# Attention scores of batches 1 to 7: zero-padded queries on all 128 rows in place of paired half-row matmuls

## The chip, the cores and the metric

One core of a Trainium2 chip runs the whole program. The metric is the device time of one execution in microseconds (us), a median of several runs. TensorE (PE) does the matmuls, ScalarE (ACT) the exponentials and part of the copies out of PSUM, VectorE (DVE) the rest of those and the elementwise work, GpSimd (POOL) casts and starts part of the DMAs, SyncE (SP) starts the other DMAs.

## What is computed

Eight batches, 12 heads, 448 positions, 64 numbers a head. Attention comes first, with one more term in the denominator; its output, with the heads side by side, is the input x (448 x 768 a batch) of a gated convolution.

```python
scores = scale * np.matmul(q, k.transpose(0, 1, 3, 2))
e = np.exp(scores - m)
attn = e / (np.sum(e, axis=-1, keepdims=True) + np.exp(-m) + 1e-09)
x = np.matmul(attn, v)                       # then (B, S, H * D)
proj = x @ w_proj                            # x1, x2, x3, 768 columns each
x2_conv = np.fft.irfft(np.fft.rfft(x2, n=S, axis=1) * H, n=S, axis=1)
out = (x1 * x2_conv * x3) @ w_out
```

## The kernel before

**Attention (L592 to L721).** The unit of work is a pair of heads, number i = 6 b + hp, so 48 in all. The two heads of a pair lie on the partitions: head u on partitions 64u to 64u+63 of `qT` and `kT`, which hold the transposed queries (448 columns a pair) and keys (four blocks of 128 columns a pair). Both are double-buffered by batch (`b % 2`). Keys are handled in four *turns* t. In turn 0 one block holds the last 64 keys of both heads, in a block-diagonal layout, so one matmul over all 128 rows gives the scores of both (L606). In turns 1 to 3 each head has 128 keys of its own, and each needs a matmul over only its 64 partitions (L604): two half-row matmuls a turn, into the two halves of one PSUM buffer `sc`. There are two such buffers. ACT takes the exponential of a whole turn (L612, L617), then TensorE multiplies by the values (L649, L654), VectorE normalises (L667 to L669), and x is transposed, by TensorE (L703) or by a DMA (L693).

**Turns in pairs.** For batches 1 to 7, turns 1 to 3 are issued two at a time by `both` (L631): of the sequence of all turns 1 to 3, each even one is joined to the one before it, so that four half-row matmuls follow each other. Such a task takes both `sc` buffers. Turn 0 also waits, in the plan, for turn 2 of the pair of heads before it. Batch 0 issues each turn alone.

**Dense part (`dense`, L724).** For each batch: folding of x on VectorE (L747 to L763), projection of the folded x2 (L781), its spectrum (L808), products with the filter's spectrum (L822, L828), the gates x1 and x3 (L854, 12 groups of 6 matmuls, copied out at L866 and L869), the inverse transform (L888), and the output projection (L949) with its copies (L961) and stores (L968).

**Input.** Batches 0 and 1 are *staged*: SP loads q, k and v in float32, VectorE (the first) or GpSimd (the others) casts q and k (L301, L295), GpSimd casts v (L308) and the shared rows (L323, L326), TensorE transposes (`turn`, L332 to L339), and VectorE copies the results to `qT` and `kT` (L356, L348). Batches 2 to 7 are *loaded*: GpSimd starts DMAs that cast on the way (q at L376, k at L384 and L386, v at L398) and then copies two blocks of v (L406, 64 partitions x 384 each); SP starts the transposing DMAs into `qT` and `kT` (L410, L415). GpSimd also starts the loads of the filter (L487 to L491) and of the weights (L582, L587), in the order of `GATES` (L168).

**Order of work.** Each engine executes its own instructions in order. That order is written by a planner (`Plan`, L42). Every task has an engine, a cost, a wanted time, what it needs and makes, and ring buffers that it takes and gives. When an engine is free in the plan's clock, the first task in order of wanted time that can start is placed next. Wanted times of attention come from `tau` (L235): 3.5 us a pair of heads in batch 0, 5.5 in batch 1, and `PERIOD` / 6 after that, from `BASE2`. Those of the dense part come from `span` (L732), which spreads a batch's work over `PERIOD`, from `READY0` and `READY1` for the first two batches. Loads of a batch from 2 on are wanted 40 us before its attention (L371). The plan decides order alone; on the chip the semaphores decide the time.

Of the kernel before, what the change touches and what calls it, by code (L numbers as in the profile page):

```python
# [15 lines left out]
BF16 = mybir.dt.bfloat16  # L16
I32 = mybir.dt.int32

B, H, S, DH = 8, 12, 448, 64
# [22 lines left out]
class Plan:  # L42
# [14 lines left out]
    def add(self, eng, cost, want, emit, need=(), make=(), take=(), give=(), dma=0.0, after=0.0):  # L57
        self.tasks.append((want, len(self.tasks), eng, cost, emit, need, make, take, give, dma, after))
# [87 lines left out]
def kernel(  # L146
# [11 lines left out]
    nc = tc.nc  # L158
# [4 lines left out]
    SLOT1 = 5.5  # L163
    BASE2 = 77.0
    READY1 = 80.0
    READY0 = 35.0
    BPS = 18.0
    GATES = ((1, ("cq", 4)), ("F", ("cv", 7)), (0, ("cv", 9)), (2, ("cv", 10)), ("O", ("cv", 11)))  # L168
    STEP = 1.5
# [2 lines left out]
    const = ctx.enter_context(tc.tile_pool(name="const", bufs=1))  # L172
# [27 lines left out]

    kT = [const.tile([128, NHP, 4, 128], BF16, name=f"kT{i}") for i in range(2)]
    qT = [const.tile([128, NHP, S], BF16, name=f"qT{i}") for i in range(2)]
    vn = [const.tile([128, NHP, 7, DH + 1], BF16, name=f"vn{i}") for i in range(2)]
    vr = [const.tile([128, NHP, 2, DH + 1], BF16, name=f"vr{i}") for i in range(2)]
    ks = const.tile([128, NHP, 128], BF16, name="ks")
# [2 lines left out]
    er = [const.tile([128, S + REM], BF16, name=f"er{i}") for i in range(2)]  # L208
# [20 lines left out]
        }  # L229
    )  # L230
    add = plan.add
    ATT0, SLOT0, PERIOD = 6.0, 3.5, 44.5
    BASE = 31.0

    def tau(i, frac=0.0):  # L235

        if i < NHP:
            return ATT0 + SLOT0 * (i + frac)
        if i < 2 * NHP:
            return BASE + SLOT1 * (i + frac - NHP)  # L240
        return BASE2 + (i + frac - 2 * NHP) * PERIOD / NHP
# [348 lines left out]
    T = {}  # L590

    def attention(i):  # L592
        b, hp = divmod(i, NHP)
        P = T.setdefault(i, {})
        P["e"] = [None] * 4
        def scores(t):
            if t or b:
                P["sc", t] = sc = psc.tile([128, 2, 512], F32, name="sc")
            else:
                P["sc", t] = sc = phy.tile([128, 1, 512], F32, name="sc0", tag="hy")  # L600
            if t:
                for u in range(2):
                    c = slice(64 * u, 64 * u + 64)
                    nc.tensor.matmul(sc[:, u, 0:S], kT[b % 2][c, hp, t, :], qT[b % 2][c, hp, :])  # L604
            else:
                nc.tensor.matmul(sc[:, 0, 0:S], kT[b % 2][:, hp, 0, :], qT[b % 2][:, hp, :])  # L606

        def exps(t):
            sc = P["sc", t]
            if t:  # L610
                P["e"][t] = e = es[(3 * i + t - 1) % 6]
                nc.scalar.activation(  # L612
                    e[:, 0 : 2 * S].rearrange("p (u n) -> p u n", u=2), sc[:, :, 0:S], AF.Exp, scale=SCALE
                )
            else:
                P["e"][t] = e = er[i % 2]
                nc.scalar.activation(e[:, 0:S], sc[:, 0, 0:S], AF.Exp, scale=SCALE)  # L617

        P["scores"] = scores
        for t in range(4):  # L620
            w = tau(i, t / 4)
            ring = "sc" if t or b else "hy"
            if t == 0 or b == 0:
                add("PE", 0.4 if t else 0.19, w, lambda t=t: scores(t),
                    need=[("kT", i), ("qT", i)] + ([("S", i - 1, 2)] if b else []),
                    make=[("S", i, t)], take=[(ring, ("S", i, t))])
            elif (3 * i + t) % 2 == 0:

                old = (i, t - 1) if t > 1 else (i - 1, 3)

                def both(pair=(old, (i, t))):  # L631
                    for j, n in pair:
                        T[j]["scores"](n)

                add("PE", 0.61, tau(old[0], old[1] / 4), both, need=[("kT", old[0]), ("qT", old[0]), ("kT", i), ("qT", i)],
                    make=[("S",) + old, ("S", i, t)], take=[("sc", ("S",) + old), ("sc", ("S", i, t))])
            add("ACT", 0.93 if t else 0.56, w - 1.0, lambda t=t: exps(t), need=[("S", i, t)],
                make=[("e", i)], take=[("e" if t else "er", (i, t))], give=[(ring, ("S", i, t))])

        def attn_out(hf):  # L640
            e = P["e"]
# [35 lines left out]
        for hf in range(2):  # L677
            w = tau(i, 1.1 + 0.4 * hf)
            add("PE", 0.48, w, lambda hf=hf: attn_out(hf),
                need=[("e", i), ("ones", b % 2), "pads"] + ([("v", i), ("vr", b)] if b < NSTAGED else [("vn", b), ("vr", b)]),  # L680
                make=[("V", i, hf)], take=[("hy" if hf and b == 0 else "op", ("V", i, hf))], give=done)
            add("DVE", 0.78, w - 0.5, lambda hf=hf: norm(hf),
                need=[("V", i, hf)] + ([("X", NHP * (b - 1) - 1)] if b >= 2 else []),
                make=[("xb", i)], give=[("hy" if hf and b == 0 else "op", ("V", i, hf))])
# [29 lines left out]
        w = tau(i, 1.7)  # L714
        on_act = 4 <= i < 6
        old = [("G", b - 2)] if b >= 2 else []
# [7 lines left out]
    def dense(b):  # L724

        L = {}
        spread = PERIOD if b < n_batches - 1 else 36.0
        ready = tau(NHP * (b + 1), 1.0) if b > 1 else (READY0, READY1)[b]
        lag = 2.5
# [279 lines left out]
    with (  # L1009
        tc.tile_pool(name="tabs", bufs=1) as tp,  # L1010
        tc.manual_schedule(engines={E.PE, E.Pool, E.DVE, E.Activation, E.SP}),
    ):
        zero1 = tp.tile([128, 1], F32, name="zero1")
        warm = tp.tile([128, 1], F32, name="warm")
        add("DVE", 0.1, -20.0, lambda: nc.vector.memset(zero1, 0.0), make=["zero1"])
        add("POOL", 1.1, -20.0, count, make=["count"])
        add("POOL", 0.6, -19.0, lambda: make_identity(nc, ident_bf), make=["ident"])
        add("DVE", 2.8, -19.0, phases, need=["count"], make=["phases"])

        def blank(to):  # L1020
            nc.scalar.copy(to, zero1[0 : to.shape[0], :].to_broadcast(list(to.shape)))

        def spin():

            t = phy.tile([128, 512], F32, name="spin", tag="hy")
            for _ in range(SPIN):
                nc.tensor.matmul(t[:, 0:128], ident_bf, ident_bf)

        add("PE", 4.0, -20.0, spin, need=["ident"], make=["spin"], take=[("hy", "spin")], give=[("hy", "spin")])
        add("ACT", 1.6, -20.0, lambda: blank(ks[:].rearrange("p g c -> p (g c)")), need=["zero1"], make=["zero ks"])  # L1030

        add("ACT", 0.8, -18.0, lambda: blank(vr[0][:].rearrange("p g u d -> p (g u d)")), need=["zero1"], make=[("zero vr", 0)])
        add("ACT", 0.6, -17.0, sines, need=["phases"], make=["sines"])
        add("ACT", 1.5, -16.0, lambda: nc.scalar.activation(warm, zero1, AF.Exp), need=["zero1", "sines"])

        def pads():
            for e in es:
                nc.gpsimd.memset(e[:, 2 * S :], 0.0)
            for e in er:
                nc.gpsimd.memset(e[:, S:], 0.0)  # L1040

        add("POOL", 0.8, 7.0, pads, make=["pads"], after=4.5)

        def ones(i):
            nc.gpsimd.memset(vn[i][:, :, :, DH : DH + 1], 1.0)
            for u in range(2):
                nc.gpsimd.memset(vr[i][64 * u : 64 * u + 64, :, u, DH : DH + 1], 1.0)

        add("DVE", 0.4, 20.0, lambda: nc.vector.memset(vr[1], 0.0), make=[("zero vr", 1)], after=12.0)
        for i in range(2):  # L1050
            add("POOL", 0.7, (6.0, 24.0)[i], lambda i=i: ones(i), need=[("zero vr", i)], make=[("ones", i)],
                after=(4.5, 16.0)[i])
        for b in range(n_batches):
            if b < NSTAGED:
                staged(b)
            else:
                loaded(b)
        add("DVE", 0.5, tau(NHP * NSTAGED) - 30.0, lambda: nc.vector.memset(kn[:, :, 0, :], 0.0),
            need=[("c" + x, g) for x in "kqv" for g in range(NHP * NSTAGED - NHP, NHP * NSTAGED)], make=["zero kn"])
        for n, (part, key) in enumerate(GATES):  # L1060
            load, size = {
                "F": (filter_load, 4.5), "O": (wout_load, 8.0),
            }.get(part, (lambda part=part: wproj_load(part), 8.0))
            add("POOL", 1.6 if part == "F" else 0.95, 12.0 + 3 * n, load,
                need=[key] + (["ft", "bps"] if part == "F" else []),
                make=[{"F": "filt", "O": "wout"}.get(part, ("w", part))],
                take=[("yT", "F")] if part == "F" else [], dma=size)
        more_tables()
        filter_spectrum()
        for i in range(n_batches * NHP):  # L1070
            attention(i)
        for b in range(n_batches):
            dense(b)
        plan.run()
# [30 lines left out]
```

## Time and profile before

| what | value |
|---|---|
| median of three runs | 404.11 us (402.27 to 405.47) |
| profiled execution, its own time | 402.27 us |
| its span, first to last instruction | 400.5 us |
| mean granted TensorE clock | 0.987 |
| half-row score matmuls (L604) | 288, busy 43.0 us |
| full-row score matmuls (L606) | 48, busy 17.8 us |
| exponentials of turns 1 to 3 (L612) | 144, mean 923 ns, busy 127.8 us |
| time that DVE waited in all for TensorE at L667 | 49.6 us |
| longest single wait of ACT for a score at L612 | 3.9 us |

How to read the profile: a busy time is the union of an engine's instructions; PEld is TensorE's weight loads, which overlap matmuls. A group is written as line, engine, operation, output<-input and its shape. In a stage table, a row gives the stretch, its length, each engine's busy time with its number of instructions in brackets, and then the granted clock, the share of the DMA engines and their rate. In a timeline a row gives the start and the length of several instructions of one kind merged (x12 is twelve of them). A row of waits gives who waited, for whom, the total in us, the number of waits and the longest. Matmul lengths are modelled, and a matmul overlaps the next one, so start times say more than lengths.

### The profile page before, as it was taken

The numbers are of one execution on the slowest core, as the hardware profiler recorded it, in microseconds if no ns is written. First come the engines' busy times: TensorE is split into PE (matmuls) and PEld (weight loads), VectorE is DVE, ScalarE is ACT, GpSimd is POOL, SyncE is SP. The second block draws the span as 40 slices with busy tenths as digits, with TensorE's granted clock in tenths as the row PEclk, the third lists the DMA queues.
The fourth block names the chain that finished last, engine by engine and source line by source line (L and its number), as shares of the span: only waits on it lengthen the run. The fifth ranks groups of instructions, "written<-read, shape, count | busy, mean of one in ns | idle before, by whom it ended". The sixth has DMA issues, their size and how long they took to land.

```text
span 400.5 us, 8959 instructions
## 1 busy us (share of the span) xinstructions
PE 384.6 (96%) x3461; PEld 245.2 (61%) x3461; DVE 257.0 (64%) x773; ACT 268.2 (67%) x461; POOL 111.3 (28%) x177
## 2 busy tenths in 40 slices
PE   7968999999999999999999999999999999999995
PEld 5545666666565566656756566656756576666562
DVE  4748778782675557775778447855678447855750
ACT  7747686733887867776677767767776767743343
POOL 5827393322813534061505204602100000000000
PEclk9977999999999999999999999999999999999999
DMA  8999999999999999999999699949820221021004
GB/s 204 229 230 233 174 176 190 152 117 182 105 133 138 215 167 124 147 83 164 153 131 96 125 200 132 105 83 179 110 41 15 119 54 28 15 77 56 0 3 157
DMA packets 179420, 50.44 MB, mean 126 GB/s; under 512 B 166126, under 2 KB 175793, under 8 KB 179377
## 3 DMA queue, kind: packets, MB, share of 16 engines
q0 software_dynamic: 101680, 17.80, 64.5%
q1 hardware_dynamic: 77696, 32.06, 42.3%
q8 instruction: 27, 0.44, 0.5%
q14 instruction: 17, 0.13, 0.1%
HBM read 43.86 MB, written 11.01 MB: 137 GB/s over the span
## 4 chain that ended last, share of the span: by engine, by line
PE 87%; DMA 6%; ACT 2%; SPq 1%; issue 1%; POOL 1%; DVE 0%; POOLq 0%; DVEq 0%; ACTq 0%
PE pps L854 27%; PE pps L781 16%; PE ops L949 12%; PE op L654 9%; PE sc L604 8%; PE cps L888 5%; DMA nat<-in_q_dram 3%; PE op L649 3%; PE xsp L808 2%; PE sc L606 2%; DMA xT<-xb 2%; DMA nat<-in_k_dram 1%; PE xps L703 1%; ACT e L612 1%; SPq L270 1%
## 5 line engine op out<-in xcount | busy, mean ns | idle before, releaser
L612 ACT ACTIVATE e<-sc 128x896 bf16<-128x896 f32 x144 | 127.8, 923 | 22.0 <-PE sc L604 21.4
L854 PE MATMUL pps<-xT,wproj_bf 128*128 128x448 bf16 x576 | 120.1, 352 | 0.6 <-ACT x L866 0.6
L854 PEld LDWEIGHTS <-wproj_bf 128*128 128x128 bf16 x576 | 54.0, 98 | 46.9 <-issue 4.8
L781 PE MATMUL pps<-wproj_bf,xf 128*113 128x384 bf16 x384 | 69.8, 328 | 1.0 <-ACT x L795 0.5
L654 PE MATMUL op<-vn,e 128*128 128x65 bf16 x1152 | 59.6, 197 | 0.8 <-ACT e L612 0.8
L781 PEld LDWEIGHTS <-xf 128*113 128x113 bf16 x384 | 48.6, 132 | 17.5 <-issue 6.6
L654 PEld LDWEIGHTS <-e 128*128 128x128 bf16 x1152 | 52.8, 100 | 6.5 <-ACT e L612 1.1
L866 ACT CAST x<-pps 128x448 bf16<-128x448 f32 x48 | 25.6, 534 | 43.2 <-PE pps L854 39.3
L949 PE MATMUL ops<-wout_bf,yT 128*128 128x384 bf16 x288 | 51.2, 326 | 0.0
L667 DVE TENSOR_SCALAR rec<-op 128x4 f32<-128x4 f32 x96 | 15.4, 160 | 50.8 <-PE op L654 49.6
L869 DVE TENSOR_TENSOR g<-x,pps 128x448 bf16<-128x448 bf16 x48 | 29.8, 620 | 24.4 <-PE pps L854 24.1
L384 POOL DMA_DIRECT2D nat<-in_k_dram x36 | 29.8, 845 | 51.6 <-DMA kT<-nat 48.6
L604 PE MATMUL sc<-qT,kT 64*128 64x448 bf16 x288 | 43.0, 370 | 0.4 <-ACT er L617 0.4
L649 PE MATMUL op<-vr,er 128*128 128x130 bf16 x192 | 43.1, 225 | 0.1
L669 DVE TENSOR_TENSOR xb<-op,rec 128x256 bf16<-128x256 f32 x96 | 40.7, 424 | 3.3
L961 ACT COPY osb<-ops 128x384 f32<-128x384 f32 x56 | 25.4, 483 | 20.8 <-PE ops L949 20.3
L949 PEld LDWEIGHTS <-yT 128*128 128x128 bf16 x288 | 26.9, 98 | 19.1 <-issue 2.1
L822 DVE TENSOR_TENSOR t<-xs,hrs 113x768 bf16<-113x768 bf16 (+1 forms) x64 | 33.5, 557 | 7.0 <-ACT xs L816 7.0
L617 ACT ACTIVATE er<-sc 128x448 bf16<-128x448 f32 x48 | 26.3, 549 | 17.2 <-PE sc L606 17.2
L816 ACT CAST xs<-xsp 113x384 bf16<-113x384 f32 (+1 forms) x64 | 28.2, 484 | 3.1 <-PE xsp L808 3.0
L795 ACT CAST x<-pps 113x384 bf16<-113x384 f32 x32 | 15.5, 486 | 18.0 <-PE pps L781 18.0
L793 DVE CAST x<-pps 113x384 bf16<-113x384 f32 x32 | 17.7, 554 | 13.4 <-PE pps L781 13.4
(104 smaller groups left out, 439.7 us busy)
## 6 DMA issues: line engine op xcount, KB each, us to landing
out_dram<-osb SPq DMA_DIRECT2D x24, 384.0 KB, 2.8
nat<-in_q_dram POOLq DMA_DIRECT2D x24, 168.0 KB, 6.8
vn<-in_v_dram POOLq DMA_DIRECT2D x6, 672.0 KB, 14.1
wproj_bf<-in_moe_w_proj_dram POOLq DMA_DIRECT2D x3, 1152.0 KB, 8.9
nat<-in_k_dram POOLq DMA_DIRECT2D x36, 96.0 KB, 3.9
nat<-in_q_dram SPq DMA_DIRECT2D x24, 112.0 KB, 4.9
nat<-in_k_dram SPq DMA_DIRECT2D x12, 192.0 KB, 4.9
nat<-in_v_dram SPq DMA_DIRECT2D x12, 192.0 KB, 5.5
```

The source lines that it names most:

```text
L384: nc.gpsimd.dma_start(kn[:, :, 1 + t, c], kr[:, :, 4 * u + t, :])
L604: nc.tensor.matmul(sc[:, u, 0:S], kT[b % 2][c, hp, t, :], qT[b % 2][c, hp, :])
L612: nc.scalar.activation(e[:, 0 : 2 * S].rearrange("p (u n) -> p u n", u=2), sc[:, :, 0:S], AF.Exp, scale=SCALE)
L649: nc.tensor.matmul(op[:, n, :, :], e[0][:, o : o + 128], vr[b % 2][:, hp, :, :], start=True, stop=False)
L654: nc.tensor.matmul(op[:, n, u, :], e[1 + t][:, u * S + o : u * S + o + 128], vn[b % 2][:, hp, 4 * u + t, :], start=False, stop=(u == 1 and ...
L669: nc.vector.tensor_tensor(W["xb", b][:, hp, 2 * hf : 2 * hf + 2, :].rearrange("p t (u d) -> p t u d", u=2), op[:, :, :, 0:DH], rec[:].unsq ...
L781: nc.tensor.matmul(pps[:FQ, :DCH], W["xf", b][:, pg, kt, 0:FQ], wproj_bf[:, kt, D + ch * DCH : D + (ch + 1) * DCH], start=(kt == 0), stop= ...
L816: nc.scalar.copy(L["xs", par, ch][:K, pg % 2, :], L["Z", pg, ch][:K, :DCH])
L822: nc.vector.tensor_tensor(t[:K], L["xs", par, ch][:K], h, op=ALU.mult)
L854: nc.tensor.matmul(p[:, :S], wproj_bf[:, kt, 2 * part * D + dt * 128 : 2 * part * D + (dt + 1) * 128], xT()[:, kt, 0:S], start=(kt == 0), ...
L869: nc.vector.tensor_tensor(g[:, dt, :], L["x1", dt], p[:, :S], op=ALU.mult)
L949: nc.tensor.matmul(ops[:n, :DCH], y[:, dt, 0:n], wout_bf[:, dt, ch * DCH : (ch + 1) * DCH], start=(dt == 0), stop=(dt == NDT - 1),)
```

## The change

For batches 1 to 7 the queries of a pair of heads are copied by GpSimd into a new tile `qz` (three of them, used in turn by i % 3): half u holds head u's queries on that head's 64 partitions and zeros on the other 64. A score matmul of turns 1 to 3 then runs over all 128 partitions, `kT` block (both heads) against half u of `qz`; the zeros take out the other head. Batch 0 keeps the half-row matmuls. The pairing of turns (`both`) and turn 0's wait in the plan are removed: each turn is a task of its own with cost 0.38, which takes one buffer. Each copy (`spread`, two for a pair of heads, 84 in all, 64 partitions x 448) needs `qT` of this pair, the zeros, and the scores of the pair three before it. Six memsets on VectorE write the zeros once, wanted from 24 us on and placed at 12 us of the plan's clock at the earliest. `PERIOD` goes from 44.5 to 46 and `READY0` from 35 to 37. `GATES` and everything else stay.

```diff
-    READY0 = 35.0
+    READY0 = 37.0
...
+    qz = [const.tile([128, 2, S], BF16, name=f"qz{i}") for i in range(3)]
...
-    ATT0, SLOT0, PERIOD = 6.0, 3.5, 44.5
+    ATT0, SLOT0, PERIOD = 6.0, 3.5, 46.0
...
+        z = qz[i % 3]
+
+        def spread(u):
+            c = slice(64 * u, 64 * u + 64)
+            nc.gpsimd.tensor_copy(z[c, u, :], qT[b % 2][c, hp, :])
+
+        halves = b == 0
+        for u in range(0 if halves else 2):
+            add("POOL", 0.68, tau(i) - 4.0 + 0.1 * u, lambda u=u: spread(u),
+                need=[("qT", i), ("zero", i % 3)] + ([("S", i - 3, 3)] if i >= 3 else []),
+                make=[("qz", i)])
...
-                    c = slice(64 * u, 64 * u + 64)
-                    nc.tensor.matmul(sc[:, u, 0:S], kT[b % 2][c, hp, t, :], qT[b % 2][c, hp, :])
+                    c = slice(64 * u, 64 * u + 64) if halves else slice(0, 128)
+                    nc.tensor.matmul(
+                        sc[:, u, 0:S], kT[b % 2][c, hp, t, :], qT[b % 2][c, hp, :] if halves else z[:, u, :]
+                    )
...
-            if t == 0 or b == 0:
-                add("PE", 0.4 if t else 0.19, w, lambda t=t: scores(t),
-                    need=[("kT", i), ("qT", i)] + ([("S", i - 1, 2)] if b else []),
-                    make=[("S", i, t)], take=[(ring, ("S", i, t))])
-            elif (3 * i + t) % 2 == 0:
-                old = (i, t - 1) if t > 1 else (i - 1, 3)
-                def both(pair=(old, (i, t))):
-                    for j, n in pair:
-                        T[j]["scores"](n)
-                add("PE", 0.61, tau(old[0], old[1] / 4), both, need=[("kT", old[0]), ("qT", old[0]), ("kT", i), ("qT", i)],
-                    make=[("S",) + old, ("S", i, t)], take=[("sc", ("S",) + old), ("sc", ("S", i, t))])
+            add("PE", 0.38 if t else 0.19, w, lambda t=t: scores(t),
+                need=[("kT", i), ("qz", i) if t and not halves else ("qT", i)], make=[("S", i, t)],
+                take=[("sc" if t or b else "hy", ("S", i, t))])
...
+        def zeros(n):
+            nc.vector.memset(qz[n][64:128, 0, :], 0.0)
+            nc.vector.memset(qz[n][0:64, 1, :], 0.0)
...
+        for n in range(3):
+            add("DVE", 0.5, 24.0 + n, lambda n=n: zeros(n), make=[("zero", n)], after=12.0)
```

More of the change, by code (lines that the diff above doesn't have):

```diff
@@ L617, in exps @@
                 nc.scalar.activation(e[:, 0:S], sc[:, 0, 0:S], AF.Exp, scale=SCALE)
-        P["scores"] = scores
         for t in range(4):
             w = tau(i, t / 4)
-            ring = "sc" if t or b else "hy"
-            if t == 0 or b == 0:
-                add("PE", 0.4 if t else 0.19, w, lambda t=t: scores(t),
-                    need=[("kT", i), ("qT", i)] + ([("S", i - 1, 2)] if b else []),
-                    make=[("S", i, t)], take=[(ring, ("S", i, t))])
-            elif (3 * i + t) % 2 == 0:
-                old = (i, t - 1) if t > 1 else (i - 1, 3)
-                def both(pair=(old, (i, t))):
-                    for j, n in pair:
-                        T[j]["scores"](n)
-                add("PE", 0.61, tau(old[0], old[1] / 4), both, need=[("kT", old[0]), ("qT", old[0]), ("kT", i), ("qT", i)],
-                    make=[("S",) + old, ("S", i, t)], take=[("sc", ("S",) + old), ("sc", ("S", i, t))])
+            add("PE", 0.38 if t else 0.19, w, lambda t=t: scores(t),
+                need=[("kT", i), ("qz", i) if t and not halves else ("qT", i)], make=[("S", i, t)],
+                take=[("sc" if t or b else "hy", ("S", i, t))])
             add("ACT", 0.93 if t else 0.56, w - 1.0, lambda t=t: exps(t), need=[("S", i, t)],
-                make=[("e", i)], take=[("e" if t else "er", (i, t))], give=[(ring, ("S", i, t))])
+                make=[("e", i)], take=[("e" if t else "er", (i, t))], give=[("sc" if t or b else "hy", ("S", i, t))])
         def attn_out(hf):
```

## The prediction

> **What bounds the kernel now.** I read the busy table, then the busy time by stage (stages cut where the profile's character changes), then the timeline of TensorE, then the waits of GpSimd. The busy table, and the stages (all instructions; then those of L604 alone, whose first figure is TensorE's):
>
> ```profile
> PE 384.6 (96%) x3461; PEld 245.2 (61%) x3461; DVE 257.0 (64%) x773; ACT 268.2 (67%) x461; POOL 111.3 (28%) x177
> ```
>
> ```profile
> 0.00:62.00 62.00, 52.81 (x554) 36.08 (x555) 41.70 (x135) 44.19 (x68) 37.94 (x94) 0.92 1.03 208
> 62.00:385.00 323.00, 321.08 (x2850) 203.18 (x2848) 211.80 (x631) 219.69 (x385) 73.35 (x84) 1.00 1.12 111
> 385.00:400.50 15.50, 10.66 (x63) 5.94 (x61) 3.50 (x10) 4.27 (x10) 0.00 (x0) 1.00 0.29 103
> ```
>
> ```profile
> 0.00:62.00 62.00, 10.77 (x56) 2.17 (x56) 0.92 1.03 208
> 62.00:385.00 323.00, 32.21 (x232) 6.78 (x232) 1.00 1.12 111
> ```
>
> From 62 to 385 us TensorE is busy 321.1 of 323 us at full clock, and the next engine, ACT, 219.7. In that stage each nanosecond of TensorE work is a nanosecond of the end; 1.9 us is all the slack. Before 62 us it has 9.2 us of holes, which loads and casts make. A modelled "busy" hides pipelining, so I price matmuls by the distance of one start to the next. The timeline of TensorE (start us, us, instruction):
>
> ```profile
> 90.82 2.43 PE L854 MATMUL pps<-xT,wproj_bf 128*128 128x448 bf16 x12
> 93.09 5.04 PE L781 MATMUL pps<-wproj_bf,xf 128*113 128x384 bf16 x30
> ...
> 102.94 0.35 PE L606 MATMUL sc<-qT,kT 128*128 128x448 bf16 x1
> 103.13 1.11 PE L854 MATMUL pps<-xT,wproj_bf 128*128 128x448 bf16 x5
> ```
>
> ```profile
> 204.83 2.43 PE L854 MATMUL pps<-xT,wproj_bf 128*128 128x448 bf16 x12
> 207.19 0.55 PE L604 MATMUL sc<-qT,kT 64*128 64x448 bf16 x4
> 207.68 0.23 PE L649 MATMUL op<-vr,er 128*128 128x130 bf16 x1
> ```
>
> First fence: twelve full-row matmuls of 448 columns take 93.09 - 90.82 = 2.27 us, 0.189 each; a full-row score (L606) also takes 103.13 - 102.94 = 0.19, weight load hidden. Second: the twelve should end at 204.83 + 2.27 = 207.10, but the half-row scores start at 207.19, 0.09 late, and hold the array until 207.68. So a pair of turns (four half-row matmuls) costs 0.09 + 0.49 = 0.58 us. The start times of all groups of four in the trace say the same: 96 ns lost at entry, 3 to 4 ns between the two halves of a turn, 196 ns to the next turn, 280 ns from the last start to the next instruction; the median sum is 580 ns, and nearly all after 103 us lie at 574 to 584.
>
> **What the skill says.** The Trainium skill, "TensorE: Matmul & The Clock Gate", section "Part 3: Packing small matmuls", says that matmuls in different row groups run at once, starts up to 4 ns apart, and that a matmul with few rows takes as long as a full one. The trace agrees: 3 to 4 ns, and 196 against 189 ns. "TensorEngine Tiling (Array Packing)", section "Key Properties", says that a change of tiling mode drains the engine. The trace agrees: 96 ns at entry, and 280 - 189 = 91 at exit. "GPSIMD Engine Reference", section "Key points", says that GpSimd shares its SBUF interfaces with VectorE; the copies of L406, 502 to 919 ns around a median of 517, fit that, but the trace names no cause.
>
> **The change, part by part.**
>
> *Scores, batches 1 to 7.* Removed: 63 pairs (7 batches x 18 turns / 2) at 0.580 us. Added: the same 252 matmuls with 128 rows, no drains: 4 x 0.189 = 0.756 a pair. Difference 0.176 x 63 = 11.1 us. The stage view checks the count: 232 half-row matmuls after 62 us are 58 pairs (10.2 us); of the 56 before it 36 are batch 0's, which keep half rows, and 20 are five pairs of batch 1 (0.9 us). Cover: none after 62 us. The 0.9 could fall into the early holes, but TensorE still has the same work to do after them, so I count it. Pairing was the whole gain of half rows: one turn alone costs 96 + 4 + 280 = 380 ns, what two full-row matmuls cost (378).
>
> *Weight loads.* A score load grows from 64 to 128 rows: 95 against 98 ns (medians of L604 and L606), hidden under 189. Nothing.
>
> *GpSimd: 84 copies of 64x448.* No row has this shape. L406, 64x384 bf16 to bf16, has a median of 517 ns; the casts L301 (512 wide, 617) and L295 (384 wide, 509) give (617 - 509) / 128 = 0.84 ns an element, so 517 + 64 x 0.84 = 571 ns, and 84 x 0.571 = 48 us; GpSimd goes from 111 to about 159 us of 416. By load this is covered by its idle time; by order it may not be, as its queue is in order. From 62 us on its waits are:
>
> ```profile
> POOL vr L406 <- DMA vn<-in_v_dram: 67.5, 6, 12.9
> POOL nat L384 <- DMA kT<-nat: 48.6, 5, 11.0
> POOL vn L398 <- issue: 23.8, 3, 11.5
> ```
>
> A copy behind such a wait is late by up to 12.9 us. Its lead: copy i may run once the last score of pair i-3 is done, and is needed by turn 1 of pair i, 2.5 pairs later. A batch takes 252.78 - 207.19 = 45.6 us between like groups, 7.6 a pair, so the lead is 19 us, 6 more than the longest wait. In batch 2 pairs follow at about 5 us (nine groups from 100.28 to 127.41), lead 12.5: about the longest wait. The copies also tie GpSimd to TensorE's progress, so loads run less far ahead; the loads of a batch are wanted 40 us before its use, and the longest median landing is 14.1 (vn), so I cost that at nothing; without this cover transposes would be late, then scores. Bounds: 0 to 6 us (12.9 + two copies and their signals, about 1.5, less 12.5 is 1.9, in up to three places); a gain is excluded, since GpSimd only gets work and later loads. I take 0.
>
> *Batch 1.* Its pairs follow their transposes at once (turn at 39.37, score at 40.75), and GpSimd also makes the casts for the next pairs. Two copies, 1.1 us plus signals, now stand between qT and turn 1, and behind a copy that waits for qT stand casts, the filter load and two weight loads. From below: 0, where TensorE has projections of batch 0 to do (from 42 us). From above: 12 copies x 0.571 = 6.9 us if each delays a cast that TensorE waits for, against 8.9 us of holes in GpSimd between 28 and 61 us. I take 0.7, half of one exposed pair of copies.
>
> *VectorE: six memsets of 64x448.* The one bf16 memset of size, L1049 (780 wide), took 708 ns, so 0.41 to 0.45 each, 2.6 us, issued early while TensorE waits for q (hole of 3.1 us at 22.5 us). Zero; up to 1 us without that cover. VectorE slowed by GpSimd's copies: 212 busy of 323 covers it.
>
> *Planner numbers and dropped order rule.* PERIOD 46 (+1.5 a batch) agrees with 9 x 0.176 = 1.6 more work a batch; READY0 and the dropped wait on the earlier score change priorities only. Single turns need one score buffer instead of two: gains at most the rare waits of pairs (0.35 us at 41.7, 0.2 at 100). Zero, from -1.
>
> **Sum.** 11.1 + 0.7 = 11.8. The profiled execution, 402.27 us (span 400.5), would give 414.1. The median before is 404.11, 1.8 above it; I forecast against the median: 415.9.
>
> **Rivals.**
> 1. *GpSimd's queue becomes a bound in batches 2 and 3*: a copy behind the wait for vn or kT comes late and TensorE, in order, stops at turn 1. For: lead 12.5 against waits of 12.9. Against: the planner puts copies ahead, and later batches have 6 us to spare. 5 us more: about 421.
> 2. *The opening suffers*: casts and weight loads of batch 1 slip behind copies; 3 to 6 us beyond the sum, 419 to 422. For: GpSimd busy 37.9 of 62 us there with casts in TensorE's path. Against: 8.9 us of holes.
> 3. *Part comes back in the opening*: single turns let ACT begin sooner and fill the 9.2 us of holes; 2 to 5 us back, 411 to 414.
> 4. *Not slower by over 1%*: the same mechanism in full. It decides from 11.8 - 4.0 = 7.8 us recovered; as the later stage has only 1.9 us of slack, at least 5.9 of the 9.2 us before 62 us must close. These wait for loads (3.1 us for q alone) that the change does not hasten. About 407.
>
> **Chances.** Forecast (413.5 to 418.5) 0.60; rival 1 0.14; rival 2 0.14; rival 3 0.07; rival 4 0.05. The range of 8 in 10, 411.5 to 422, leaves out rival 4, the worst ends of 1 and 2, and the low end of 3. About 1% is what a measurement here can tell from no change: slower 0.95, same 0.04, faster 0.01.
>
> **What would show it.** Right: scores of batches 1 to 7 stand as 128-row matmuls, start to start 0.189, two a turn; TensorE from 62 us to the tail about 10 us longer and still over 98% busy; GpSimd's copies near 0.57 us; at most about 1 us of waits of scores for qz. Wrong: full-row scores not near 0.189, holes in TensorE before turn 1 of a pair that end on GpSimd's copies, or an opening whose gate matmuls (L854) start over 3 us later than at 60.6 us.

## The result, and the profile after

The changed kernel takes 420.9 us (median of four runs, 417.71 to 422.54) against 403.69 before; the ratio is 1.0414, interval 1.0335 to 1.0494: slower by 17.2 us. The profiled execution took 419.84 us, its span is 418.0, against 400.5 before.

The busy table of after, its stages (columns as before), and the two waits of TensorE that are new in kind or size:

```profile
PE 393.4 (94%) x3461; PEld 263.7 (63%) x3461; DVE 272.0 (65%) x779; ACT 272.3 (65%) x461; POOL 162.2 (39%) x261
```

```profile
0.00:62.00 62.00, 50.03 (x548) 35.97 (x549) 43.30 (x137) 44.49 (x67) 42.20 (x101) 0.92 0.98 200
62.00:100.00 38.00, 32.66 (x268) 20.23 (x266) 25.17 (x71) 17.58 (x32) 17.98 (x24) 0.96 1.85 121
...
190.00:235.00 45.00, 45.00 (x403) 30.43 (x402) 31.60 (x89) 32.44 (x55) 20.22 (x28) 1.00 1.19 121
```

```profile
PE sc L618 <- POOL qz L601: 5.1, 2, 4.9
PE tps L339 <- POOL q L302: 4.5, 2, 3.7
```

TensorE is full in the steady stage, as before. But it loses 5.3 of 38 us between 62 and 100 us, where before it lost 0.3, and the waits name one stop of 4.9 us for a query copy. The same stretch in the kernel before:

```profile
62.00:100.00 38.00, 37.72 (x315) 24.30 (x313) 24.89 (x72) 20.42 (x38) 11.12 (x13) 1.00 2.03 157
```

The groups of instructions and the start times price the two sides of the forecast:

```profile
L601 POOL COPY qz<-qT 64x448 bf16<-64x448 bf16 x84 | 51.8, 616 | 132.0 <-PE sc L618 111.4
...
L618 PE MATMUL sc<-qz,kT 128*128 128x448 bf16 x252 | 67.9, 355 | 5.9 <-POOL qz L601 5.1
```

Nearly all full-row turns after 109 us take 376 to 381 ns from start to start (0.189 a matmul); the copies have a median of 561 ns. The timeline of TensorE around the stop, and of GpSimd at the same time:

```profile
67.19 0.35 PE L657 MATMUL op<-vn,e 128*128 128x65 bf16 x6
72.46 1.90 PE L618 MATMUL sc<-qz,kT 128*128 128x448 bf16 x4 [4.92 <-POOL qz L601]
74.16 0.84 PE L811 MATMUL xsp<-x,ft 113*112 113x384 bf16 x2
74.80 1.64 PE L857 MATMUL pps<-xT,wproj_bf 128*128 128x448 bf16 x6
76.27 0.54 PE L618 MATMUL sc<-qz,kT 128*128 128x448 bf16 x2
```

```profile
56.40 0.83 POOL L588 DMA_DIRECT2D wout_bf<-in_moe_w_out_dram  x1
57.22 3.74 POOL L377 DMA_DIRECT2D nat<-in_q_dram  x4
60.94 1.65 POOL L385 DMA_DIRECT2D nat<-in_k_dram  x2
64.32 0.82 POOL L385 DMA_DIRECT2D nat<-in_k_dram  x1 [1.73 <-DMA wproj_bf<-in_moe_w_proj_dram]
70.14 0.67 POOL L387 DMA_DIRECT2D nat<-in_k_dram  x1 [5.00 <-DVE xf L761]
71.02 0.82 POOL L385 DMA_DIRECT2D nat<-in_k_dram  x1 [0.20 <-issue]
71.84 1.19 POOL L601 COPY qz<-qT 64x448 bf16<-64x448 bf16 x2
```

The copy for pair 10 (71.84) stands behind two k loads of batch 2, and the first of them waits 5.0 us. The same load waits as long in the kernel before, where nothing urgent stood behind it:

```profile
POOL nat L386 <- DVE t L822: 5.0, 1, 5.0
```

Both views name VectorE as the releaser. But VectorE wrote the zeros that this load needs at 57.4 us, long before. In the trace the load waits on semaphore 117 as well, one of eight (111 to 118) that GpSimd's DMAs use in turn to tell of their landing. The DMA eight places earlier, also on 117, is the load of the output weights (issued 56.40); its last part landed at 69.61 and the wait ended at 69.64. Before, landing and end of the wait are 67.09 and 67.11. So the suspect is that landing, which the experiments test.

After the stop TensorE is slow for a while: six gate matmuls take 76.27 - 74.80 = 1.47 us instead of 1.13, and the stage table of after gives a granted clock of 0.57 (the first figure behind the last bracket):

```profile
72.00:76.00 4.00, 3.45 (x11) 1.51 (x11) 0.00 (x0) 2.29 (x4) 3.84 (x7) 0.57 2.21 159
76.00:80.00 4.00, 4.00 (x35) 2.27 (x33) 2.74 (x6) 2.07 (x4) 2.48 (x2) 1.00 2.59 138
```

That is 4 x 0.43 = 1.7 us more, an estimate from these two rows.

### The profile page after: what moved, and what is told of

It reads as the page before. It is cut to its first block, busy times and chain, and to the rows that moved or that the text cites. A ratio compares the mean times of both kernels' runs of the same rounds, so it can differ in the third digit from the quotient of the medians.

```text
span 418.0 us, 9124 instructions
## 1 busy us (share of the span) xinstructions
PE 393.4 (94%) x3461; PEld 263.7 (63%) x3461; DVE 272.0 (65%) x779; ACT 272.3 (65%) x461; POOL 162.2 (39%) x261
## 4 chain that ended last, share of the span: by engine, by line
PE 82%; DVE 8%; DMA 4%; ACT 2%; POOL 1%; SPq 1%; issue 1%; POOLq 0%; ACTq 0%
PE pps L857 25%; PE pps L784 14%; PE ops L952 13%; PE sc L618 11%; PE op L657 7%; DMA nat<-in_q_dram 4%; PE cps L891 4%; PE op L652 2%; PE xsp L811 2%; PE sc L622 2%; DVE xf L761 1%; DVE xb L672 1%; DVE uw L550 1%; DVE cv L911 1%; DVE u L756 1%
## 5 line engine op out<-in xcount | busy, mean ns | idle before, releaser
L628 ACT ACTIVATE e<-sc 128x896 bf16<-128x896 f32 x144 | 129.9, 920 | 37.7 <-PE sc L618 36.6
L857 PE MATMUL pps<-xT,wproj_bf 128*128 128x448 bf16 x576 | 121.5, 353 | 0.6 <-ACT x L869 0.6
L601 POOL COPY qz<-qT 64x448 bf16<-64x448 bf16 x84 | 51.8, 616 | 132.0 <-PE sc L618 111.4
L857 PEld LDWEIGHTS <-wproj_bf 128*128 128x128 bf16 x576 | 55.7, 98 | 49.8 <-issue 2.5
L618 PE MATMUL sc<-qz,kT 128*128 128x448 bf16 x252 | 67.9, 355 | 5.9 <-POOL qz L601 5.1
L784 PE MATMUL pps<-wproj_bf,xf 128*113 128x384 bf16 x384 | 70.9, 326 | 1.6 <-DVE xf L761 0.8
L784 PEld LDWEIGHTS <-xf 128*113 128x113 bf16 x384 | 49.9, 132 | 16.4 <-issue 1.5
L825 DVE TENSOR_TENSOR t<-xs,hrs 113x768 bf16<-113x768 bf16 (+1 forms) x64 | 38.0, 628 | 12.4 <-ACT xs L819 12.4
L618 PEld LDWEIGHTS <-kT 128*128 128x128 bf16 (+1 forms) x288 | 22.5, 97 | 18.2 <-issue 9.1
```

The costliest lines, as they stand in the source:

```text
L601: nc.gpsimd.tensor_copy(z[c, u, :], qT[b % 2][c, hp, :])
L628: nc.scalar.activation(e[:, 0 : 2 * S].rearrange("p (u n) -> p u n", u=2), sc[:, :, 0:S], AF.Exp, scale=SCALE)
L784: nc.tensor.matmul(pps[:FQ, :DCH], W["xf", b][:, pg, kt, 0:FQ], wproj_bf[:, kt, D + ch * DCH : D + (ch + 1) * DCH], start=(kt == 0), stop= ...
L825: nc.vector.tensor_tensor(t[:K], L["xs", par, ch][:K], h, op=ALU.mult)
L857: nc.tensor.matmul(p[:, :S], wproj_bf[:, kt, 2 * part * D + dt * 128 : 2 * part * D + (dt + 1) * 128], xT()[:, kt, 0:S], start=(kt == 0), ...
```

## The experiments

Medians, each with its ratio to the kernel before on the same chip; that kernel's median was 403.38 us for experiments 1, 4, 5 and 6 and 404.27 for 2, 3, 7 and 8. "Spans" are those of the profiled executions.

**1. copies_first.** Batch 2's loads wait, in the plan, for the copies of pair 11.

```diff
         room = ["zero kn" if b == NSTAGED else ("turn", b - 1)]
+        if b == NSTAGED:
+            room = room + [("qz", i0 - 1)]
```

> The kernel after, with one change: all loads of batch 2 stand in GpSimd's queue behind the query copies of pairs 10 and 11. Theory (two costs: 11.1 us for the lost pairing, and 5 to 6.5 us for one stop of TensorE, whose copy for pair 10 stands behind a load that waits): the 4.9 us stop goes, time about 414.5 to 415.5 us, that is 11 to 12 above before. Rival A (the extra 6 us come from the copies' load on GpSimd and VectorE everywhere): stays at 419 to 421. Rival B (the loads of batch 2 are themselves on the path, so that moving them back costs as much as it gains): 419 or more, with a new hole of TensorE near the start of batch 2.

Measured: 408.98 us, 1.0149 (1.0123 to 1.0174), 5.6 above before and 12 below after. The stop is gone:

```profile
62.00:100.00 38.00, 37.76 (x309) 25.01 (x308) 24.66 (x72) 19.28 (x36) 21.33 (x28) 1.00 1.90 133
```

Rivals A and B fall: all 84 copies are still there. But the theory's number is wrong by 6 us too: without the stop the loss is half of the 11.1 forecast by medians (two thirds by spans). See the next section.

**2. kload_late.** The two k loads that need VectorE's zeros go behind the load of v, for batch 2.

```diff
-                add("POOL", 0.85, want + STEP * n, lambda u=u, t=t: k_load(u, t), need=room,
-                    make=[("kn", b)], dma=1.0, after=start + STEP * n)
+                late = 24.0 if b == NSTAGED and t == 3 else 0.0
+                add("POOL", 0.85, want + STEP * n + late, lambda u=u, t=t: k_load(u, t), need=room,
+                    make=[("kn", b)], dma=1.0, after=start + STEP * n + (want + late if late else 0.0))
```

> The kernel after, with the two k loads of batch 2 that need VectorE's zeros (L387) moved in GpSimd's queue behind the load of v; the eighth DMA after the load of the output weights is then a k load that needs no zeros. Theory D (that place in the queue waits for the landing of the output weights, the DMA eight before it on the same of eight semaphores): the stop of TensorE at pair 10 stays, 4 to 5.5 us, time 418 to 422. Rival Z (the load waits for VectorE, as the table of waits names it): the stop goes, 409 to 412.

Measured: 423.59 us, 1.0481 (1.0423 to 1.054). The stop stays, 4.7 us. The load now in that place needs no zeros, waits nearly as long (4.75 us), and here the profile names the right releaser. The time is 1.6 us above the range of theory D; a lower clock explains about as much: it is granted as 0.73, 0.50 and 0.92 in the three stretches of 4 us from 68 us on, an estimated 4 x (0.27 + 0.50 + 0.08) = 3.4 us, against 1.7 in after. GpSimd's timeline:

```profile
55.44 0.82 POOL L589 DMA_DIRECT2D wout_bf<-in_moe_w_out_dram  x1
...
68.91 0.82 POOL L385 DMA_DIRECT2D nat<-in_k_dram  x1 [4.75 <-DMA wout_bf<-in_moe_w_out_dram]
69.72 1.19 POOL L602 COPY qz<-qT 64x448 bf16<-64x448 bf16 x2
```

**3. wout_later.** Only the load of the output weights moves, behind the copies of pair 11.

```diff
-                need=[key] + (["ft", "bps"] if part == "F" else []),
+                need=[key] + (["ft", "bps"] if part == "F" else [("qz", 11)] if part == "O" else []),
```

> The kernel after, with only the load of the output weights moved in GpSimd's queue behind the copies of pairs 10 and 11; the loads of batch 2 keep their order. Theory D (the stop ends with the landing of the output weights): the stop shrinks to what the landing of the last gate weights leaves, under 1 us, time 409 to 412, unless the output weights now come late for the first output projection at about 85 us (then up to 3 us more). Rival Z (the wait is for VectorE's zeros): stop stays, 418 to 422.

Measured: 409.68 us, 1.0136 (1.009 to 1.0183): the stop goes although batch 2's loads keep their places. The k load now in that place still waits, but 2.1 us (the DMA eight before it is the last load of gate weights; it landed at 62.58, and the wait on its semaphore ended at 62.60, so VectorE is again named wrongly). The copies come early enough that TensorE does not stop for them:

```profile
63.11 0.68 POOL L387 DMA_DIRECT2D nat<-in_k_dram  x1 [2.07 <-DVE x L796]
63.89 0.82 POOL L385 DMA_DIRECT2D nat<-in_k_dram  x1
64.70 1.19 POOL L601 COPY qz<-qT 64x448 bf16<-64x448 bf16 x2
```

Moving the loads that need the zeros leaves the stop; moving the load of the output weights removes it. Theory D holds, rival Z falls.

**4. single_half.** No copies, no zeros; half rows everywhere, each turn alone.

```diff
-        halves = b == 0
+        halves = True
...
-        for n in range(3):
-            add("DVE", 0.5, 24.0 + n, lambda n=n: zeros(n), make=[("zero", n)], after=12.0)
```

> The kernel after, but with half-row scores in all batches, each turn alone, and no copies, no zeros. Theory (pairing was the whole gain of half rows; a turn alone costs 96 + 4 + 280 = 380 ns against 378 for two full-row matmuls): 11.3 us above before, about 415. Rival (half rows are cheaper than full rows even alone, and padding is what costs): 404 to 408.

Measured: 412.2 us, 1.0241 (1.0206 to 1.0276): 8.8 above before, 2.5 short of the number, and the rival's 404 to 408 is out. Lone half rows are no cheaper than full rows. The stretch from the first spectrum matmul (`xsp`) of batch 2 to that of batch 6 shows it; in every kernel here it holds the scores of 36 pairs of turns and the same other matmuls. Before (pairs), copies_first (full rows) and single_half:

```profile
150.17:328.89 178.72, 178.70 (x1638) 113.41 (x1635) 117.76 (x356) 127.93 (x221) 40.56 (x47) 1.00 1.10 115
151.59:335.51 183.92, 183.92 (x1633) 124.09 (x1632) 127.16 (x356) 130.55 (x220) 69.78 (x95) 1.00 1.08 114
151.53:337.33 185.80, 185.80 (x1634) 115.72 (x1632) 117.97 (x356) 130.87 (x220) 40.38 (x47) 1.00 0.96 109
```

TensorE is busy all the time in all three, so the differences are its own work. They repeat: 178.7 us also in plan_numbers (experiment 6), 183.9 to 184.4 in all six kernels with full rows there. A lone half-row turn costs (185.80 - 183.92) / 72 = 0.026 us more than a full-row one, not the 0.002 of the prediction (380 against 378 ns).

**5. unread_copies.** The kernel before, plus the copies, which nothing reads.

```diff
+    qz = [const.tile([128, 2, S], BF16, name=f"qz{i}") for i in range(3)]
...
+        z = qz[i % 3]
+        def spread(u):
+            c = slice(64 * u, 64 * u + 64)
+            nc.gpsimd.tensor_copy(z[c, u, :], qT[b % 2][c, hp, :])
+        for u in range(2 if b else 0):
+            add("POOL", 0.68, tau(i) - 4.0 + 0.1 * u, lambda u=u: spread(u),
+                need=[("qT", i)] + ([("S", i - 3, 3)] if i >= 3 else []), make=[("qz", i)])
```

> The kernel before, with paired half-row scores, plus the 84 query copies on GpSimd in about the places that they have in the kernel after; nothing reads them. Theory (GpSimd's copies cost nothing by their load, only when TensorE waits for one): 0 to 1 us above before. Rival A (load on GpSimd, contention with VectorE, later loads): 4 to 6 us above before.

Measured: 411.36 us, 1.0214 (1.0187 to 1.0241). My 0 to 1 us was wrong: 8 us (9.0 by spans) without TensorE waiting for a copy once. Part of it is a stop of 2.6 us with a lower clock after it. Its timeline:

```profile
139.68 1.00 SPq L979 DMA_DIRECT2D out_dram<-osb  x2
...
143.57 0.86 ACT L972 COPY osb<-ops 128x384 f32<-128x384 f32 x2 [3.00 <-DMA out_dram<-osb]
...
144.31 1.75 ACT L623 ACTIVATE e<-sc 128x896 bf16<-128x896 f32 x2
...
145.30 0.53 PE L617 MATMUL sc<-qT,kT 128*128 128x448 bf16 x1 [2.62 <-ACT e L623]
```

ACT waited for an output buffer, which the stores to `out_dram` free; its exponentials stood behind that wait, and TensorE behind those. The stores left SP's queue at 139.68 us (at 135.71 before, where the opening is 2.8 us shorter), behind transposes of later loads; that the copies had pushed these back is likely and was not tested. From batch 1's to batch 2's first spectrum the kernel takes 56.90 us against 52.21, 4.7 more. The stop and the clock after it make an estimated 4.3 of them (2.6, and 4 x (0.09 + 0.34) = 1.7 for a granted 0.91 and 0.66 from 142 to 150 us). Another 2.8 us lie in the opening, and 1.6 in batches 2 to 5, of which TensorE stood idle 1.2 (busy 179.08 of 180.29). What makes up the last two isn't settled: contention and later loads (rival A) are not excluded there. copies_first has the same number of copies without this stop, so a fixed price of a copy is not its cause.

**6. plan_numbers.** `READY0` 37 and `PERIOD` 46 in the kernel before.

> The kernel before with READY0 37 and PERIOD 46 only. Theory (these change the order of ready work, not its amount, on an engine that is full): within 1 us of before. Rival C (the new order explains the 6 us beyond the lost pairing): 4 to 6 us above before.

Measured: 402.99 us, 0.9991 (0.998 to 1.0001). Rival C falls.

**7. batch1_half.** Batch 1 on lone half rows too, copies from batch 2 on (`halves = b <= 1`, and the wait on the pair three before from i = 15 on).

> The kernel after, with batch 1 also on half rows, each turn alone, so that the first copies are those of batch 2. Theory (nothing in batch 1 stands behind the waiting load any more; a lone half-row turn costs about 0.40 us with its aftermath, 18 of them 0.4 us more than full rows): no stop, 409 to 411.5. Rival (copies cost by their load everywhere): 72 of 84 copies are left, 417 or more.

Measured: 412.66 us, 1.0206 (1.0151 to 1.0261). No stop at pair 10, as expected, and the rival's 417 is out; the time is 1 us above the stated range and 3.3 by spans above copies_first. Lone half rows explain 0.5 of that (18 turns at 0.026). Of the 3.3 us, 2.7 lie before batch 1's first spectrum; their cause was not followed.

**8. paired_full.** copies_first, with the old `both` around full-row turns (cost 0.76).

> The kernel with the copies of pairs 10 and 11 ahead of batch 2's loads, and its full-row turns again issued two at a time, as the half-row turns before: grouping without concurrency. Theory (what was lost is the concurrency of the two row groups): the same as without grouping, 408 to 411. Rival G (the grouped order itself was worth the time, through ACT and the buffers): 402 to 405.

Measured: 415.34 us, 1.0267 (1.0225 to 1.0309): grouping alone gains nothing, so rival G falls. It even loses time against copies_first (ratio 1.0267 against 1.0149; 4.0 us by spans), outside the theory's range. Batches 2 to 5 are nearly as in copies_first (184.39 us against 183.92). Of the 4.0 us, 3.4 lie before batch 1's first spectrum, where TensorE stops for 2.7 us, from 49.9 to 52.6, until VectorE has normalised an earlier result (`xb`, L687). Whether the grouping brings this stop about is open.

## Why the prediction was right or wrong

The range (411.5 to 422) held and the direction was right. That the range held is in part luck: two errors of opposite sign met in it. The mechanism that was forecast, full-row scores without a stop, takes 408.98 us (experiment 1), below the range; a stop that the working put at nothing brought the time back into it. By spans the 17.5 us are about 7.3 for the scores, 4.9 for the stop, 1.7 for the clock after it, and 3.6 that the runs explain only in part (below).

**Scores (forecast 11.1): too large.** Direction and cause are right. A full-row turn costs 378 to 380 ns, and grouping without concurrency gains nothing (experiment 8). The size is not. copies_first, which has all of the change but the stop, is 5.6 us above before by medians, 7.3 by spans (407.8 - 400.5; the profiled execution of before is the fastest of its four). All of the 7.3 arises after batch 1: its first spectrum starts at 97.97 us before and at 97.94 in copies_first, with the same matmuls done. So the 1.6 us of batch 1's nine pairs do not show. They can have fallen into the opening's holes, which I had considered and rejected; they can also be hidden in the opening's own spread, since plan_numbers, with half rows in pairs, reaches this point only at 100.02 us. And in batches 2 to 5 a pair of turns costs (183.92 - 178.72) / 36 = 0.144 us more, not 0.176. Most of the difference is an aftermath that I left out of the 0.58: in the trace of before, the second instruction after a group of four also starts late, by 12 ns in the median and 23 in the mean, so a group costs about 0.60 us, and full rows 0.154 more. The last 0.01 is open; it is not idle time of TensorE, which is full there in both kernels.

**GpSimd's queue (forecast 0): wrong, and the main error.** The list of waits that I showed left out the fourth row, L386 with 5.0 us, which decided. I compared lead and wait only for batches 2 and 3 and only for the waits on v and kT; the stop came one place earlier, at pair 10 of batch 1. There the copy's `qT` is ready at 63.2 us, and TensorE wants the copy at 67.5, so the lead is 4.3 us, not 12.5. For batch 1 I had asked what stands behind a copy, not what stands ahead of it: here three k loads, of which two wait, until 64.0 and until 69.6. Rival 1 had the mechanism and the size of the stop (5 us) but the wrong place; that its total of about 421 fits is luck, since it stands on the 11.1 for the scores; rival 2 had the place, but spoke of casts. Between the profiled executions of after and copies_first lie 418.0 - 407.8 = 10.2 us. Of these 4.9 are the hole and 1.7 the clock after it, which the working had no term for; 1.9 are already there at batch 0's first spectrum (58.40 against 56.46 us), and up to 57 us every engine does the same instructions in the same order in both, so probably this is spread between runs; the rest, 1.7, are smaller waits up to 150 us.

**Batch 1 (forecast 0.7):** the copies there cost nothing that can be seen once the stop is gone. **Memsets (0):** right; six of 0.245 us each, shorter than my 0.41 to 0.45. **VectorE slowed (0):** right for the time, though it is slowed (below). **Planner numbers (0):** right as far as experiment 6 shows, which changed them in the kernel before. **Length of a copy (0.571):** 0.561 in the median, 0.616 in the mean.

## What to carry to other kernels

Price an array-tiling mode by the distance of starts from before its entry to two instructions after its exit; it pays here only because two turns share one entry and exit. When work is put on an engine that also starts DMAs, read every wait in its queue, short ones too, and ask for each new instruction what stands ahead of it and when its own input arrives: a wait that hurt nobody becomes a stop of the bound engine. A stop can also cost the clock after it: 1.7 us after the stops of 4.9 us (after) and 2.6 us (unread_copies), 3.4 after that of 4.7 us (kload_late), all estimates from the granted clock, but nothing after the 2.7 us of paired_full, where the granted clock stays 1.00 from 48 to 60 us.

## What the runs showed that I had not expected

In these traces a DMA started by GpSimd waited for the landing of the DMA eight before it, whatever the data: the load of the output weights so holds up the DMA eight places behind it (5.0 us in after, 4.75 us in experiment 2).

Several of VectorE's operations with two inputs in SBUF are much longer while a copy runs on GpSimd. In copies_first the products L827 take 778 ns in the median where they overlap a copy (19 of them) and 551 where they do not (45); the sums L913 739 against 384. The multiplication L674, which reads PSUM, stays at 425 against 424. But so does L928 (`yT`), with two inputs in SBUF, at 559 against 558, though only 4 of them overlap a copy. The Trainium skill, "GPSIMD Engine Reference", section "Key points", says that the two engines contend in VectorE's instructions with two inputs in SBUF; the trace agrees for L827 and L913, not for L928. VectorE had the room here: TensorE stayed full in batches 2 to 5 of copies_first.
